# Score matmuls with a selector as the stationary operand, over keys transposed as fp32 pairs, in a decode attention kernel

## The chip, the cores and the metric

The kernel runs on one core of one Trainium2 chip. The metric is the device time of one execution in microseconds. A trace is of one execution: two traces whose loops run the same code differ by 0.12 us per pair, so smaller differences between traces say nothing.

## The reference

Two branches, mixed by a gate. Nearly all the time goes to the attention branch: 2 batches x 32 heads, one query each, 16384 keys of 128 elements.

```python
q = (x @ wq).reshape(B, 1, 32, 128).transpose(0, 2, 1, 3)
scores = einsum("bhqd,bhkd->bhqk", q, k_cache) * 128 ** -0.5
p = softmax(scores)
o = einsum("bhqk,bhkd->bhqd", p, v_cache)
a = o.transpose(0, 2, 1, 3).reshape(B, 1, 4096) @ wo
b = mixer_mlp(x)                      # small: 2 rows through four weights
return g * a + (1 - g) * b            # g = sigmoid(sum(x * gate_w))
```

K and V together are 537 MB; with the weights the kernel reads 572.5 MB.

A warning on "correct": the comparison with the reference says little about the score path, and I don't use it as proof that a re-ordered score layout is right.

## The kernel before: the parts that matter

The kernel is written engine by engine, with semaphores; the code below is abridged to what matters here. The 64 head-batch pairs `i` go one after another. A pair has 4 K pieces and 4 V pieces of 1 MB each, loaded into a ring of 16 slots; a load for a slot is issued by SP once the slot's former piece has been used up. K pieces alternate between two paths (`KPATH = "pd"`).

Path "p" (TensorE): 8 transposes per group, ScalarE evicts the group, and 8 score matmuls with the keys as the stationary operand follow two groups later (`QKLAG = 2`).

```python
for g in range(GPP):                             # 4 groups of 8 rows per piece
    for cc in range(8):                          # waits for the eviction 3 groups before (3 PSUM banks)
        e.transpose(bank_b(bank, cc*128, ...), slot_ap(s, r*DH, (r+1)*DH), ident_bf)
    act: activation(kt_f32(kts), tps_f32(bank), Copy)        # 128 x 512 fp32 words
    pending_qk.append(...); flush_qk(QKLAG)
ring_free[jp] = last transpose                   # the K slot may be loaded again
# issue_qk: 8 x matmul(S_ps[:, c:c+NQ], lhsT=kt(cc), rhs=qsb[:, i:i+NQ], start=True, stop=True)
# after the last group: 2 x activation(ssb, S_ps, Copy)
```

Path "d" (VectorE): `prd = K * qrep` (`qrep` is the pair's query, copied to all 128 partitions) in two instructions, then two reduces over the 128 elements, straight to the scores `ssb`.

The softmax of a pair closes the loop, because the next pair's `qrep` and evictions stand behind this pair's exp in ScalarE's queue:

```python
dve : tensor_reduce(M_P, ssb, max)                        # waits for all four pieces
pool: partition_all_reduce(GMAX, M_P, max)
pool: tensor_scalar(NBIAS, GMAX, -scale, mult)
act : activation(ptile, ssb, Exp, bias=NBIAS, scale=scale, accum_out=L_P)
pool: partition_all_reduce(LSUM, L_P, add)
# then, next pair:  act: qrep copy, evictions ...   dve: prd <- ring, qrep
```

PV matmuls (the product of the softmax with V: 4 columns of `ptile` stationary, 512 columns of V moving) run five pieces behind, on TensorE, between the K groups.

Of the kernel before, what the change touches and what calls it, by code (L numbers as in the profile page):

```python
# [3 lines left out]
F32 = mybir.dt.float32  # L4
BF16 = mybir.dt.bfloat16
# [53 lines left out]
def build_kernel(nc, A_x, A_k_cache, A_v_cache, A_wq, A_wo, B_x, B_w1, B_w2, B_w3, B_w4,  # L59
# [10 lines left out]
    DSPLIT = cfg.get("DSPLIT", 2)  # L70
    PSPLIT = cfg.get("PSPLIT", 4)
    NPRD2 = cfg.get("NPRD2", 2)
    NT = 3
    VG = 4

# [14 lines left out]
    NPC = SK // PKEYS  # L90
    NCH = SK // 128
    GPP = R // 8
    assert NCH + NQ <= 512 and R % VG == 0
    NPB = LAG // NPC + 2
    assert D <= PE_ELEMS and Fdim <= PE_ELEMS and H * DH <= PE_ELEMS
    S_TOK = Sq
# [8 lines left out]
    ident_bf = nc.alloc_sbuf_tensor("ident_bf", [128, 128], BF16)  # L105
    ident_f = nc.alloc_sbuf_tensor("ident_f", [128, 128], F32)
    qsb = nc.alloc_sbuf_tensor("qsb", [128, NPAIR + NQ], BF16)
    ptile = nc.alloc_sbuf_tensor("ptile", [128, NPB * NCH], BF16)
    ssb = nc.alloc_sbuf_tensor("ssb", [128, NPB * NCH], F32)
    st = nc.alloc_sbuf_tensor("st", [128, NPB * 8], F32)  # L110
# [47 lines left out]
    def bank_f(b, c0, c1):  # L158
        return ps[:, b * 512 + c0: b * 512 + c1]

    def bank_b(b, c0, c1):
        return psb[:, b * 1024 + c0: b * 1024 + c1]

    def S_ps(i):
        return bank_f(3 + (i % 2), 0, NCH + NQ)
    qrow_ps = bank_b(0, 512, 640)[0:NPAIR, :]
    qrep_ps = bank_f(7, 0, 128)
    O4_ps = ps[0:VG, 5 * 512: 6 * 512]
    AT_ps = bank_f(6, 0, W)
# [51 lines left out]
    def ring_dma(src_ap, dst_view=None, width=PE_ELEMS):  # L221
# [20 lines left out]
    t_identf = P.op("pool", lambda e: e.affine_select(  # L242
        out=ident_f[:], in_=ident_f[:], compare_op=ALU.not_equal, fill=1.0, base=0,
        pattern=[[-1, 128]], channel_multiplier=1), [t_identf])
    t_ar0 = P.op("pool", lambda e: e.memset(arscr[:], 0.0))
    t_ar0 = P.op("pool", lambda e: e.partition_all_reduce(arscr[:, 1:2], arscr[:, 0:1], channels=128,
                                                         reduce_op=RED.add), [t_ar0])
# [36 lines left out]
    def matmul_T(pieces, ncols, nk, n_out_tiles, out_ps, rhs_fn, extra_waits, width_b=Bsz):  # L284
        waits = [ring_loaded[j] for (j, s, t0, nt) in pieces] + list(extra_waits)
        last = None
        first = True
        for nt_i in range(n_out_tiles):
            for t in range(nk):
                lhs, j = wtile(pieces, ncols, t, nt_i * 128, (nt_i + 1) * 128)  # L290
                is_last = (nt_i == n_out_tiles - 1 and t == nk - 1)
                last = P.op("pe", (lambda e, o=out_ps[:, nt_i * width_b:(nt_i + 1) * width_b], l=lhs,
                                   r=rhs_fn(t), st_=(t == 0), sp_=(t == nk - 1):
                                   e.matmul(o, lhsT=l, rhs=r, start=st_, stop=sp_)),  # L294
                            waits if first else (), track=is_last)
                first = False
        for (j, s, t0, nt) in pieces:
            ring_free[j] = last
        return last
# [3 lines left out]
    w1p = load_weight_rows(B_w1, KT, D, per_piece_D)  # L303
    w2p = load_weight_rows(B_w2, KT, D, per_piece_D)

    t_QT = matmul_T(wqp, H * DH, KT, H, QT_ps, lambda t: xT_bf[:, t * Bsz:(t + 1) * Bsz], [t_xTbf])
    t_qsb = P.op("dve", lambda e: e.tensor_copy(qsb[:, 0:NPAIR], QT_ps), [t_QT])
    off = NPAIR
    while off < NPAIR + NQ:
        wdt = min(NPAIR, NPAIR + NQ - off)  # L310
        t_qsb = P.op("dve", lambda e, off=off, wdt=wdt: e.tensor_copy(qsb[:, off:off + wdt], qsb[:, 0:wdt]),
                     [t_qsb])
        off += wdt
    t_qrowp = P.op("pe", lambda e: e.transpose(qrow_ps, qsb[:, 0:NPAIR], ident_bf[:]), [t_qsb, t_ident])
    t_qrow = P.op("dve", lambda e: e.tensor_copy(qrow[:], qrow_ps), [t_qrowp])
    w3p = load_weight_rows(B_w3, KT, Fdim, max(1, PE_ELEMS // Fdim))

    t = P.op("dve", lambda e: e.tensor_tensor(
        v3(gp[:]), v3(xT_f[:]), gwT_f[:].unsqueeze(2).broadcast_to([128, KT, Bsz]), ALU.mult),
        [t_xTf, t_gwTf])  # L320
# [26 lines left out]
        return t10  # L347

    t_ln1 = layernorm_T(xT_f, t_xTf, ln_s[0])
    lnT = ln_s[0]["out"]  # L350
    t_hT = matmul_T(w1p, D, KT, KT, hT_ps, lambda t: lnT[:, t * Bsz:(t + 1) * Bsz], [t_ln1])
    t_u1 = P.op("act", lambda e: e.activation(u1T[:], hT_ps, ACTF.Gelu_apprx_tanh), [t_hT])
# [33 lines left out]
        stream.append(("V", n))  # L386

    def kpath(n):
        return KPATH[n % len(KPATH)]

    evac_tk = {}
# [42 lines left out]
    def softmax(i):  # L434
# [11 lines left out]
        pooladd_tk[i] = P.op("pool", lambda e: e.partition_all_reduce(  # L446
            stc(j, LSUM), stc(j, L_P), channels=128, reduce_op=RED.add), [exp_tk[i], prev(rl_tk, i, NPB)])

    def issue_qk(gd):
        i, pc, g, n, kts = gd  # L450
        j = i % NPB
        waits = [evac_tk[n]]
        if not qk_started.get(i):
            qk_started[i] = True
            waits += prev_list(sread_tk, i, 2) + [t_qsb]
        last = None
        for cc in range(8):
            c = pc * R + g * 8 + cc
            last = P.op("pe", (lambda e, o=S_ps(i)[:, c:c + NQ], l=kt_ap(kts, cc * 128, (cc + 1) * 128),
                               r=qsb[:, i:i + NQ]: e.matmul(o, lhsT=l, rhs=r, start=True, stop=True)),  # L460
                        waits if cc == 0 else (), track=(cc == 7))
        qk_tk[n] = last
        if g == GPP - 1:
            pe_done.setdefault(i, []).append(pc)
            if len(pe_done[i]) == sum(1 for q in range(NPC) if kpath(i * NPC + q) == "p"):
                for pcq in pe_done[i]:
                    c0 = pcq * R
                    tk = P.op("act", (lambda e, o=S_sb(j)[:, c0:c0 + R], a=S_ps(i)[:, c0:c0 + R]:
                                      e.activation(o, a, ACTF.Copy)), [last, prev(exp_tk, i, NPB)])  # L469
                    sread_tk.setdefault(i, []).append(tk)  # L470
                for tk in list(sread_tk[i]):
                    add_part(i, tk)

    qk_started = {}
    pe_done = {}

    def flush_qk(keep):
# [28 lines left out]
    def finish(i):  # L506
# [17 lines left out]
        if b == Bsz - 1:  # L524
            pending_A.append(h)

    def k3(ap, nr):
        return ap.rearrange("p (r d) -> p r d", d=DH)

    for (kind, n) in stream:  # L530
# [11 lines left out]
        if kind == "K":  # L542
            path = kpath(n)
            if pc == 0 and any(kpath(i * NPC + q) != "p" for q in range(NPC)):
                make_qrep(i)
            if path == "p":
                for g in range(GPP):
                    gn = gcount[0]
                    gcount[0] += 1
                    bank = gn % NT  # L550
                    kts = gn % NKT
                    waits = []
                    if g == 0:
                        waits.append(ring_loaded[jp])
                    if gn >= NT:
                        waits.append(evac_tk[gn - NT])
                    if gn == 0:
                        waits += [t_qsb, t_ident, t_qrow]
                    last = None
                    for cc in range(8):  # L560
                        r = g * 8 + cc
                        last = P.op("pe", (lambda e, o=bank_b(bank, cc * 128, (cc + 1) * 128),
                                           a=slot_ap(s, r * DH, (r + 1) * DH): e.transpose(o, a, ident_bf[:])),  # L563
                                    waits if cc == 0 else (), track=(cc == 7))
                    tT_tk[gn] = last
                    ev = EVAC[gn % len(EVAC)]
                    ew = [tT_tk[gn], prev(qk_tk, gn, NKT)]
                    if ev == "d":
                        evac_tk[gn] = P.op("dve", lambda e, o=kt_f32(kts), a=tps_f32(bank): e.tensor_copy(o, a), ew)
                    else:  # L570
                        evac_tk[gn] = P.op("act", lambda e, o=kt_f32(kts), a=tps_f32(bank):
                                           e.activation(o, a, ACTF.Copy), ew)  # L572
                    pending_qk.append((i, pc, g, gn, kts))
                    flush_qk(QKLAG)
                ring_free[jp] = tT_tk[gcount[0] - 1]
            else:
# [19 lines left out]
                                ([ring_loaded[jp], qrep_tk[i]] + wfree) if q_ == 0 else ())  # L596
                    qrep_users[i].append(last)
                ring_free[jp] = last
                rsd = R // DSPLIT
                red = None  # L600
                for q_ in range(DSPLIT):
                    red = P.op("dve", (lambda e, o=scols[:, q_ * rsd:(q_ + 1) * rsd],
                                       a=k3(dst_ap[:, q_ * rsd * DH:(q_ + 1) * rsd * DH], rsd):
                                       e.tensor_reduce(o, a, AX.X, ALU.add)),  # L604
                               ([last, prev(exp_tk, i, NPB)]) if q_ == 0 else ())
                if path == "d":
                    prd_free[0] = red
                else:
# [4 lines left out]
        else:  # L613
# [3 lines left out]
            last = None  # L617
            ngq = R // VG
            for gq in range(ngq):
                c0 = pc * R + gq * VG  # L620
                is_last = (gq == ngq - 1)
                last = P.op("pe", (lambda e, l=P_ap(j, c0, c0 + VG),
                                   rr=slot_ap(s, gq * VG * DH, (gq + 1) * VG * DH),
                                   st_=(c0 == 0), sp_=(c0 == NCH - VG):
                                   e.matmul(O4_ps, lhsT=l, rhs=rr, start=st_, stop=sp_)),  # L625
                            waits if gq == 0 else (), track=is_last)
            ring_free[jp] = last
# [86 lines left out]
```

## Time and profile before

Median 2014.72 us (2013.1 to 2017.89, 4 runs).

The page's first part: busy time of each engine, with its share of the span.

```profile
span 2011.3 us, 26961 instructions
PE 1100.0 (55%) x11908; PEld 659.2 (33%) x11908; DVE 1176.9 (59%) x675; ACT 394.2 (20%) x971; POOL 72.7 (4%) x207
```

No engine is over 60% busy. The chain that ended last, by engine and by line, says why: a third of the span is "issue", time for which the profile shows no wait.

```profile
DVE 57%; issue 33%; POOL 2%; ACT 2%; PE 2%; DMA 2%; SPq 1%; DVEq 0%; POOLq 0%
DVE prd L595 28%; DVE ssb L604 28%; ACT ptile L443 2%; SPq L231 1%; POOL st L438 1%; DMA ring<-in_A_wq_dram 1%; POOL st L441 1%; DVE st L436 1%; PE ps L625 1%; DMA ring<-in_B_w_dram 1%; PE ps L294 1%; ACT qrep L501 1%; DVEq L50 0%; DVE st L510 0%; POOLq L441 0%
```

The costliest groups (line, engine, operation, out<-in, shape, count | busy us, mean ns of one | idle before and what ended it):

```profile
L595 DVE TENSOR_TENSOR prd<-ring,qrep 128x2048 f32<-128x2048 bf16 x256 | 575.1, 2288 | 716.3 <-ACT qrep L501 709.2
L604 DVE TENSOR_REDUCE ssb<-prd 128x16 f32<-128x2048 f32 x256 | 573.3, 2281 | 4.4
L460 PE MATMUL ps<-qsb,ktr 128*128 128x32 bf16 x4096 | 173.3, 183 | 798.3 <-ACT ktr L572 798.3
L625 PE MATMUL ps<-ring,ptile 128*4 128x512 bf16 x2048 | 595.7, 444 | 21.3 <-ACT ptile L443 21.3
L572 ACT ACTIVATE ktr<-ps 128x512 f32<-128x512 f32 x512 | 277.1, 597 | 211.3 <-PE ps L563 210.5
L563 PE MATMUL ps<-ident_bf,ring 128*128 128x128 bf16 x4096 | 306.9, 234 | 0.0
L441 POOL TENSOR_SCALAR st<-st 128x1 f32<-128x1 f32 x64 | 18.0, 281 | 632.9 <-issue 632.9
```

The last line: GpSimd's little tensor_scalar of 128x1 is idle 632.9 us in front of it, for "issue". At the end of each all-reduce of the maximum, and after each tensor_scalar, the trace has two MODIFY_POOL_CONFIG, 260 in all. These are the lines for them (line, engine, count, duration in ns, first and last start):

```profile
L441 POOLq MODIFY_POOL_CONFIG  x128: 83/83/85, 103.6 to 1985.8; - x128
L446 POOLq MODIFY_POOL_CONFIG  x128: 11/11/11, 113.0 to 1993.5; - x128
```

The way back, from the tensor_scalar to the all-reduce of the sum, is idle for 6.18 us on average, but nothing waits for that one. One pair in the timeline (start us, us, engine line operation, idle before):

```profile
1005.40 0.40 ACT L443 ACTIVATE ptile<-ssb,st 128x128 bf16<-128x128 f32 x1 [15.77 <-POOL st L441]
...
1006.16 4.49 DVE L595 TENSOR_TENSOR prd<-ring,qrep 128x2048 f32<-128x2048 bf16 x2 [11.17 <-ACT qrep L501]
1007.91 0.33 SPq L231 DMA_DIRECT2D ring<-in_A_k_cache_dram  x1
...
1011.45 0.33 SPq L231 DMA_DIRECT2D ring<-in_A_v_cache_dram  x1
...
1021.98 0.28 ACT L469 ACTIVATE ssb<-ps 128x32 f32<-128x32 f32 x2 [1.95 <-PE ps L460]
...
1024.41 0.29 DVE L436 TENSOR_REDUCE st<-ssb 128x1 f32<-128x128 f32 x1
...
1024.80 0.37 POOL L438 PARTITION_ALL_REDUCE st<-st  x1 [12.77 <-DVE st L510]
1036.63 0.26 POOL L441 TENSOR_SCALAR st<-st 128x1 f32<-128x1 f32 x1 [11.46 <-issue]
```

Read it as a loop. Exp at 1005.40; VectorE's four multiplies and reduces; the maximum at 1024.41; the all-reduce; then 11.46 us of nothing; the tensor_scalar at 1036.63 and exp again. TensorE's scores of this pair are copied at 1021.98, 2.4 us before the maximum: that path is not on the chain, but close.

The means over pairs 2 to 61 (the gap, here and below, over 3 to 61), from the trace's instructions and data packets:

| per pair, us | before |
|---|---|
| exp to exp | 30.12 (29.07 to 31.52) |
| exp to end of TensorE's score copy | 15.21 (13.66 to 17.05) |
| exp to end of VectorE's last reduce | 18.88 |
| exp to start of the maximum | 19.02 |
| all-reduce to tensor_scalar ("the gap") | 10.07 |
| exp to end of the last K/V packet | 27.09 |

In the last two pairs, with no load in flight during the gap, it is 6.76 and 7.06 us.

### The profile page before, as it was taken

The numbers are of one execution on the slowest core, as the hardware profiler recorded it, in microseconds if no ns is written. First come the engines' busy times: TensorE is split into PE (matmuls) and PEld (weight loads), VectorE is DVE, ScalarE is ACT, GpSimd is POOL, SyncE is SP. The second block draws the span as 40 slices with busy tenths as digits, with TensorE's granted clock in tenths as the row PEclk, the third lists the DMA queues.
The fourth block names the chain that finished last, engine by engine and source line by source line (L and its number), as shares of the span: only waits on it lengthen the run. The fifth ranks groups of instructions, "written<-read, shape, count | busy, mean of one in ns | idle before, by whom it ended". The sixth has DMA issues, their size and how long they took to land.

```text
span 2011.3 us, 26961 instructions
## 1 busy us (share of the span) xinstructions
PE 1100.0 (55%) x11908; PEld 659.2 (33%) x11908; DVE 1176.9 (59%) x675; ACT 394.2 (20%) x971; POOL 72.7 (4%) x207
## 2 busy tenths in 40 slices
PE   2454564564564564565465564565465465465466
PEld 2432332332332342332242332343243233233233
DVE  0375575575575575575575575575575575575573
ACT  1121121121121121121121121121121122121221
POOL 0010000000000000000000000000000000000000
PEclk9977777776776777777776777776777786777787
DMA  9997766776776776776776776776776776776670
GB/s 384 407 420 280 308 274 263 310 283 260 309 280 262 305 287 253 313 282 269 296 292 251 310 282 257 309 299 255 298 305 253 289 313 252 288 301 264 282 277 1
DMA packets 86645, 574.29 MB, mean 286 GB/s; under 512 B 9216, under 2 KB 9216, under 8 KB 19968
## 3 DMA queue, kind: packets, MB, share of 16 engines
q1 hardware_dynamic: 86528, 572.57, 71.6%
q8 instruction: 93, 1.52, 0.3%
q14 instruction: 24, 0.20, 0.0%
HBM read 572.53 MB, written 0.00 MB: 285 GB/s over the span
## 4 chain that ended last, share of the span: by engine, by line
DVE 57%; issue 33%; POOL 2%; ACT 2%; PE 2%; DMA 2%; SPq 1%; DVEq 0%; POOLq 0%
DVE prd L595 28%; DVE ssb L604 28%; ACT ptile L443 2%; SPq L231 1%; POOL st L438 1%; DMA ring<-in_A_wq_dram 1%; POOL st L441 1%; DVE st L436 1%; PE ps L625 1%; DMA ring<-in_B_w_dram 1%; PE ps L294 1%; ACT qrep L501 1%; DVEq L50 0%; DVE st L510 0%; POOLq L441 0%
## 5 line engine op out<-in xcount | busy, mean ns | idle before, releaser
L595 DVE TENSOR_TENSOR prd<-ring,qrep 128x2048 f32<-128x2048 bf16 x256 | 575.1, 2288 | 716.3 <-ACT qrep L501 709.2
L460 PE MATMUL ps<-qsb,ktr 128*128 128x32 bf16 x4096 | 173.3, 183 | 798.3 <-ACT ktr L572 798.3
L625 PE MATMUL ps<-ring,ptile 128*4 128x512 bf16 x2048 | 595.7, 444 | 21.3 <-ACT ptile L443 21.3
L604 DVE TENSOR_REDUCE ssb<-prd 128x16 f32<-128x2048 f32 x256 | 573.3, 2281 | 4.4
L460 PEld LDWEIGHTS ps<-qsb,ktr 128*128 128x128 bf16 x4096 | 146.1, 101 | 879.2 <-ACT ktr L572 808.9
L572 ACT ACTIVATE ktr<-ps 128x512 f32<-128x512 f32 x512 | 277.1, 597 | 211.3 <-PE ps L563 210.5
L563 PE MATMUL ps<-ident_bf,ring 128*128 128x128 bf16 x4096 | 306.9, 234 | 0.0
L563 PEld LDWEIGHTS ps<-ident_bf,ring 128*128 128x128 bf16 x4096 | 259.0, 105 | 39.5 <-issue 35.0
L625 PEld LDWEIGHTS ps<-ring,ptile 128*4 128x4 bf16 x2048 | 170.9, 93 | 303.2 <-issue 150.5
L443 ACT ACTIVATE ptile<-ssb,st 128x128 bf16<-128x128 f32 x64 | 25.7, 401 | 937.3 <-POOL st L441 937.3
L516 PE MATMUL ps<-ident_f,od 4*128 4x1 f32 x512 | 68.7, 251 | 19.1 <-ACT od L513 16.6
L513 ACT ACTIVATE od<-ps 4x512 f32<-4x512 f32 x64 | 37.6, 587 | 184.5 <-PE ps L625 184.5
L516 PEld LDWEIGHTS ps<-ident_f,od 4*128 4x128 f32 x512 | 63.3, 190 | 26.6 <-ACT od L513 26.6
L438 POOL PARTITION_ALL_REDUCE st<-st x64 | 25.5, 398 | 856.0 <-DVE st L510 799.8
L469 ACT ACTIVATE ssb<-ps 128x32 f32<-128x32 f32 x128 | 18.3, 195 | 120.7 <-PE ps L460 120.7
L441 POOL TENSOR_SCALAR st<-st 128x1 f32<-128x1 f32 x64 | 18.0, 281 | 632.9 <-issue 632.9
L446 POOL PARTITION_ALL_REDUCE st<-st x64 | 25.7, 401 | 396.4 <-issue 307.2
L521 ACT ACTIVATE otb<-ps,st 128x1 bf16<-128x1 f32 x64 | 16.9, 264 | 74.5 <-PE ps L516 72.2
L436 DVE TENSOR_REDUCE st<-ssb 128x1 f32<-128x128 f32 x64 | 18.3, 286 | 11.6 <-ACT ssb L469 3.0
L372 DVE TENSOR_TENSOR bT<-x1T_f,ps 128x16 f32<-128x16 f32 x1 | 0.2, 172 | 35.6 <-PE ps L294 35.6
L501 ACT ACTIVATE qrep<-ps 128x128 bf16<-128x128 f32 x64 | 16.4, 256 | 19.6 <-PE ps L499 19.6
L510 DVE RECIPROCAL st<-st 128x1 f32<-128x1 f32 x64 | 9.8, 153 | 14.3 <-POOL st L446 14.3
(71 smaller groups left out, 118.3 us busy)
## 6 DMA issues: line engine op xcount, KB each, us to landing
ring<-in_A_k_cache_dram SPq DMA_DIRECT2D x256, 1024.0 KB, 7.8
ring<-in_A_v_cache_dram SPq DMA_DIRECT2D x256, 1024.0 KB, 7.6
ring<-in_B_w_dram SPq DMA_DIRECT2D x11, 1024.0 KB, 19.6
ring<-in_A_wq_dram SPq DMA_DIRECT2D x8, 1024.0 KB, 11.9
wor<-in_A_wo_dram SPq DMA_DIRECT2D x32, 256.0 KB, 7.7
ring<-in_B_w_dram SPq DMA_DIRECT2D x8, 896.0 KB, 15.3
x<-in_A_x_dram SPq DMA_DIRECT2D x1, 4.0 KB, 1.5
gw<-in_gate_w_dram SPq DMA_DIRECT2D x1, 2.0 KB
```

The costliest lines, as they stand in the source:

```text
L436: mx_tk[i] = P.op("dve", lambda e: e.tensor_reduce(stc(j, M_P), S_sb(j), AX.X, ALU.max), part_tk[i] + [prev(poolmax_tk, i, NPB)])
L438: poolmax_tk[i] = P.op("pool", lambda e: e.partition_all_reduce(stc(j, GMAX), stc(j, M_P), channels=128, reduce_op=RED.max), [mx_tk[i], pr ...
L441: nbias_tk[i] = P.op("pool", lambda e: e.tensor_scalar(stc(j, NBIAS), stc(j, GMAX), -scale, None, ALU.mult), [poolmax_tk[i], prev(exp_tk, ...
L443: exp_tk[i] = P.op("act", lambda e: e.activation(P_ap(j, 0, NCH), S_sb(j), ACTF.Exp, bias=stc(j, NBIAS), scale=scale, accum_out=stc(j, L_P ...
L460: r=qsb[:, i:i + NQ]: e.matmul(o, lhsT=l, rhs=r, start=True, stop=True)),
L513: ocopy_tk[i] = P.op("act", lambda e: e.activation(odj, O4_ps, ACTF.Copy), [pvlast_tk[i], prev(osum_tk, i, NPB)])
L516: osum_tk[i] = P.op("pe", (lambda e, m=m: e.matmul(oT_ps, lhsT=odj[:, m * 128:(m + 1) * 128], rhs=ident_f[0:VG, m:m + 1], start=(m == 0), ...
L563: a=slot_ap(s, r * DH, (r + 1) * DH): e.transpose(o, a, ident_bf[:])),
L572: e.activation(o, a, ACTF.Copy), ew)
L595: last = P.op(eng, (lambda e, o3=o3, i3=i3, qb3=qb3: e.tensor_tensor(o3, i3, qb3, ALU.mult)), ([ring_loaded[jp], qrep_tk[i]] + wfree) if q ...
L604: e.tensor_reduce(o, a, AX.X, ALU.add)),
L625: e.matmul(O4_ps, lhsT=l, rhs=rr, start=st_, stop=sp_)),
```

## The change

The intent: fewer, larger TensorE instructions for the scores. Two neighbouring bf16 rows are seen as one row of fp32 words, so one fp32 transpose moves two rows: 4 transposes per group for 8. The eviction untangles even and odd elements. The query then becomes the stationary operand, in a 32-column window that puts it into one pair of output rows ("selector"), and 512 key columns move; 2 accumulating matmuls per group for 8. The scores come out as 32x512 and need a ScalarE copy, four transposes and two strided copies. Because the score columns now come in another order, VectorE's reduces (4 smaller ones per piece) and PV's operands are strided to match. The last six K pieces all go to TensorE (`TAILP = 6`). The diff is abridged.

```diff
-for cc in range(8): e.transpose(bank_b(...), slot_ap(s, r*DH, (r+1)*DH), ident_bf)
+for t4 in range(4): e.transpose(bank_f(bank, t4*128, ...), slot_ap(s, r*DH, (r+2)*DH).bitcast(F32), ident_f)
-evac: activation(kt_f32(kts), tps_f32(bank), Copy)
+evac: activation(kt "j par tp", bank_b "j (tp par) -> j par tp", Copy)     # 1024 bf16, source step 2
-for cc in range(8): matmul(S_ps(i)[:, c:c+NQ], lhsT=kt(cc), rhs=qsb[:, i:i+NQ], start=True, stop=True)
+for par in range(2):
+    matmul(ST_ps(i), lhsT=wbuf[:, base+30-2*Gp : base+62-2*Gp], rhs=kt(par*512, (par+1)*512),
+           start=(first and par == 0), stop=(is_last_group and par == 1))
 # after a pair's last group
-2 x activation(ssb, S_ps, Copy)
+activation(stsb, ST_ps(i), Copy)                       # 32 x 512
+4 x transpose(Sp_ps, stsb(t4), ident_f[0:32, 0:32])
+2 x activation(ssb strided, Sp_ps strided, Copy)
 # VectorE piece
-for q_ in range(DSPLIT): tensor_reduce(ssb[16], prd[16*128])               # 2 x 2048
+for g_ in range(GPP):    tensor_reduce(ssb strided [4, 2], prd[8*128])     # 4 x 1024
 def kpath(n):
+    if n >= NKP - TAILP: return "p"
     return KPATH[n % len(KPATH)]
+make_w(i): 2 x activation(wbuf window, qe/qo columns, Copy)                # after qrep, each pair
 ... (start-up: selectors psel, qe, qo; PV operands strided; order of the start-up)
```

Within the loop, the order of the instructions around them is the same as before.

## The prediction

> **What bounds it now.** 64 head-batch pairs run one after another; the pairs 2 to 61 take 30.1 us each (29.1 to 31.5, start of one exp to the next). The chain of waits shows the loop: exp, qrep (ScalarE), then VectorE 18.1 us (two K pieces, each 2 multiplies and 2 reduces of 2.24 us), max reduce, partition all-reduce on GpSimd, an "issue" gap before the GpSimd tensor_scalar of 10.05 us on average, tensor_scalar, exp. [...] the trace has two MODIFY_POOL_CONFIG per pair, and gaps of 6.8 and 7.1 us in the last two pairs, where no cache traffic is left. So I read 3 us of the gap as contention with K/V loads, which saturate the queues for some 22 us per pair and end 7.3 us into the gap.
>
> TensorE and ScalarE are off the chain, but not by much: the last PE-path score copy ends 15.2 us after exp (13.7 to 17.0), VectorE's maximum starts at 19.0. Slack 3.8 us, in odd pairs only 2 to 3.5.
>
> **What changes, per pair.**
> - VectorE: 4 reduces of 1024 for 2 of 2048. [...] +0.43 us, on the chain.
> - ScalarE eviction: 128x1024 bf16 for 128x512 fp32. The trace has 597 ns[...]. It delays the first scores after exp, with two small selector copies, by 0.7 us, and the second piece by 0.5.
> - TensorE scores: 2 matmuls of 512 columns for 8 of 32. PV's 512-column matmul takes 0.43 us cold, 0.236 warm: 0.86/0.47 us per group for 0.43/0.36. About +1.5 us.
> - Transposes: 4 fp32 for 8 bf16. The lone fp32 transpose in the tail takes 0.38 us, the bf16 one 0.32, [...] no large change (-0.5 to +1 us).
> - New before the maximum: 32x512 copy, four transposes, two strided copies instead of two plain ones: +1.4 us.
>
> The PE path thus ends near 19.6 us after exp (odd pairs 21, even 18) against VectorE's 19.45: it becomes the later one in odd pairs. The maximum comes 0.4 us (even) to 2 us (odd) later, 1.2 on average. Slots come free about 1.5 us later too, so the loads end later and the gap doesn't shrink. About +1.35 us x 61 = +82 us. The tail (last three VectorE pieces moved to TensorE) I expect to cost 10 us rather than save, as 16 evictions and their groups plus PV exceed VectorE's 19 us. Start-up: unchanged.
>
> **Predicted: 2105 us, 2045 to 2190.** Faster by over 2%: 0.03; within 2%: 0.17; slower: 0.80.
>
> **What would show it.** Right: reduces of about 1.2 us; [...] period near 31.4 us; the maximum's wait in odd pairs ended by ScalarE's score copy, not VectorE's reduce; gap still near 10 us; granted clock little changed. Wrong: PE path still ending before VectorE (then only +30 us); gap below 9 us.
>
> **What would make it wrong.** [...] load timing that changes the gap by 1 us (60 us in all); a tail that gains.

## The result

Median 2073.31 us (2064.23 to 2081.49, 10 runs) against 2015.13 us (16 runs) of the kernel before: ratio 1.0293, 95% interval 1.0276 to 1.0311. The change is slower. Ratios here are the mean time of one kernel's fast runs over that of the other's from the same rounds, so not quite the ratio of the medians quoted.

The profile after, the same parts of the page:

```profile
span 2068.7 us, 17839 instructions
PE 1262.2 (61%) x7119; PEld 631.0 (31%) x7119; DVE 1165.9 (56%) x917; ACT 666.9 (32%) x1177; POOL 74.1 (4%) x213
...
DVE 39%; issue 33%; PE 17%; ACT 6%; POOL 2%; DMA 2%; SPq 1%; POOLq 0%; DVEq 0%
DVE ssb L685 19%; DVE prd L676 19%; PE ps L710 7%; PE ps L514 5%; PE ps L643 2%; ACT ktr L653 2%; ACT ptile L477 2%; SPq L242 1%; POOL st L472 1%; PE ps L588 1%; DMA ring<-in_A_wq_dram 1%; DVE st L470 1%; POOL st L475 1%; DMA ring<-in_B_w_dram 1%; PE ps L314 1%
...
L676 DVE TENSOR_TENSOR prd<-ring,qrep 128x2048 f32<-128x2048 bf16 x250 | 561.6, 2288 | 724.7 <-ACT wbuf L491 718.2
L514 PE MATMUL ps<-ktr,wbuf 128*32 128x512 bf16 x1048 | 347.8, 439 | 666.2 <-ACT ktr L653 666.2
L685 DVE TENSOR_REDUCE ssb<-prd 128x8 f32<-128x1024 f32 x500 | 574.8, 1211 | 4.3
L653 ACT ACTIVATE ktr<-ps 128x1024 bf16<-128x1024 bf16 x524 | 500.2, 1024 | 186.8 <-PE ps L643 186.2
L710 PE MATMUL ps<-ring,ptile 128*4 128x512 bf16 x2048 | 541.4, 412 | 16.1 <-ACT ptile L477 16.1
L643 PE MATMUL ps<-ident_f,ring 128*128 128x128 f32 x2096 | 317.6, 298 | 0.0
...
L475 POOL TENSOR_SCALAR st<-st 128x1 f32<-128x1 f32 x64 | 17.4, 272 | 651.4 <-issue 651.4
```

A third fewer instructions (17839 for 26961), and TensorE is busier: the score matmuls cost 347.8 us for 173.3, and the half as many transposes 317.6 for 306.9. ScalarE's evictions went from 277.1 to 500.2 us. The chain's TensorE part (17%, 2% before) is not the end of the kernel alone: a_tail0 below, without the tail move, still has 16%. It is there because in some pairs the score copy now ends after VectorE, and the chain then runs through TensorE for the whole pair.

One pair in the timeline:

```profile
1028.97 0.40 ACT L477 ACTIVATE ptile<-ssb,st 128x128 bf16<-128x128 f32 x1 [12.68 <-POOL st L475]
...
1029.73 4.49 DVE L676 TENSOR_TENSOR prd<-ring,qrep 128x2048 f32<-128x2048 bf16 x2 [11.62 <-ACT wbuf L491]
1030.78 1.04 PE L514 MATMUL ps<-ktr,wbuf 128*32 128x512 bf16 x2 [11.37 <-ACT ktr L653]
1031.75 1.12 PE L643 MATMUL ps<-ident_f,ring 128*128 128x128 f32 x4
1032.89 0.33 SPq L242 DMA_DIRECT2D ring<-in_A_k_cache_dram  x1
...
1035.80 0.33 SPq L242 DMA_DIRECT2D ring<-in_A_v_cache_dram  x1
...
1047.30 0.29 ACT L536 ACTIVATE ssb<-ps 128x32 f32<-128x32 f32 x2 [0.52 <-PE ps L527]
...
1048.22 0.29 DVE L470 TENSOR_REDUCE st<-ssb 128x1 f32<-128x128 f32 x1
...
1058.54 0.26 POOL L475 TENSOR_SCALAR st<-st 128x1 f32<-128x1 f32 x1 [9.57 <-issue]
```

Here too the score copy (1047.30 to 1047.59) still ends before the maximum starts (1048.22). But SP issues the first load 3.92 us after exp, for 2.51 before, since the eviction and the first score group ahead of it got longer; the first V load comes at 6.83 us, for 6.05.

| per pair, us (means of pairs 2 to 61) | before | after |
|---|---|---|
| exp to exp | 30.12 | 30.73 |
| exp to end of TensorE's score copy | 15.21 | 18.86 (later than VectorE in 18 of 60 pairs) |
| exp to end of VectorE's last reduce | 18.88 | 19.11 |
| exp to start of the maximum | 19.02 | 19.33 |
| the gap | 10.07 | 10.35 |
| exp to issue of the 1st / 2nd / 8th cache load | 2.49 / 5.92 / 16.76 | 3.92 / 7.42 / 20.39 |
| exp to end of the last K/V packet | 27.09 | 28.50 |

The 57.4 us between the two profiled spans divide as follows, from the exp times in the two traces: +4.1 us up to the second pair's exp (there the maximum waits 7.03 us for the score copy), +36.4 us in the 60 pairs of the loop, +17.4 us in the last two pairs (33.3 and 38.0 us for 26.8 and 27.1), -0.5 us after them.

The last two pairs, where all or nearly all pieces are on TensorE: VectorE's maximum waits for the score copies.

```profile
2004.63 0.29 DVE L470 TENSOR_REDUCE st<-ssb 128x1 f32<-128x128 f32 x1 [15.05 <-ACT ssb L536]
...
2042.93 0.29 DVE L470 TENSOR_REDUCE st<-ssb 128x1 f32<-128x128 f32 x1 [37.94 <-ACT ssb L536]
```

### The profile page after: what moved, and what is told of

Its sections match the earlier page's. It is cut to its first block, busy times and chain, and to the rows that moved or that the text cites. A ratio compares the mean times of both kernels' runs of the same rounds, so it can differ in the third digit from the quotient of the medians.

```text
span 2068.7 us, 17839 instructions
## 1 busy us (share of the span) xinstructions
PE 1262.2 (61%) x7119; PEld 631.0 (31%) x7119; DVE 1165.9 (56%) x917; ACT 666.9 (32%) x1177; POOL 74.1 (4%) x213
## 4 chain that ended last, share of the span: by engine, by line
DVE 39%; issue 33%; PE 17%; ACT 6%; POOL 2%; DMA 2%; SPq 1%; POOLq 0%; DVEq 0%
DVE ssb L685 19%; DVE prd L676 19%; PE ps L710 7%; PE ps L514 5%; PE ps L643 2%; ACT ktr L653 2%; ACT ptile L477 2%; SPq L242 1%; POOL st L472 1%; PE ps L588 1%; DMA ring<-in_A_wq_dram 1%; DVE st L470 1%; POOL st L475 1%; DMA ring<-in_B_w_dram 1%; PE ps L314 1%
## 5 line engine op out<-in xcount | busy, mean ns | idle before, releaser
L514 PE MATMUL ps<-ktr,wbuf 128*32 128x512 bf16 x1048 | 347.8, 439 | 666.2 <-ACT ktr L653 666.2
L685 DVE TENSOR_REDUCE ssb<-prd 128x8 f32<-128x1024 f32 x500 | 574.8, 1211 | 4.3
L653 ACT ACTIVATE ktr<-ps 128x1024 bf16<-128x1024 bf16 x524 | 500.2, 1024 | 186.8 <-PE ps L643 186.2
L710 PE MATMUL ps<-ring,ptile 128*4 128x512 bf16 x2048 | 541.4, 412 | 16.1 <-ACT ptile L477 16.1
L514 PEld LDWEIGHTS ps<-ktr,wbuf 128*32 128x32 bf16 x1048 | 82.2, 99 | 794.7 <-ACT ktr L653 718.4
L643 PE MATMUL ps<-ident_f,ring 128*128 128x128 f32 x2096 | 317.6, 298 | 0.0
L643 PEld LDWEIGHTS ps<-ident_f,ring 128*128 128x128 f32 x2096 | 244.2, 150 | 116.0 <-issue 111.6
L522 ACT ACTIVATE stsb<-ps 32x512 f32<-32x512 f32 x64 | 37.6, 587 | 104.6 <-PE ps L514 104.6
L527 PE MATMUL ps<-ident_f,stsb 32*128 32x32 f32 x256 | 27.5, 227 | 43.7 <-ACT stsb L522 43.7
L527 PEld LDWEIGHTS ps<-ident_f,stsb 32*128 32x128 f32 x256 | 20.5, 136 | 75.3 <-ACT stsb L522 75.3
L475 POOL TENSOR_SCALAR st<-st 128x1 f32<-128x1 f32 x64 | 17.4, 272 | 651.4 <-issue 651.4
```

The costliest lines, as they stand in the source:

```text
L475: nbias_tk[i] = P.op("pool", lambda e: e.tensor_scalar(stc(j, NBIAS), stc(j, GMAX), -scale, None, ALU.mult), [poolmax_tk[i], prev(exp_tk, ...
L514: e.matmul(ST_ps(i), lhsT=l, rhs=r, start=st_, stop=sp_)),
L527: tk = P.op("pe", (lambda e, t4=t4: e.transpose(Sp_ps[:, t4 * 32:(t4 + 1) * 32], stj[:, t4 * 128:(t4 + 1) * 128], ident_f[0:32, 0:32])), ( ...
L643: e.transpose(o, a, ident_f[:])),
L653: evac_tk[gn] = P.op("act", lambda e, o=o_pl, a=a_pl: e.activation(o, a, ACTF.Copy), ew)
L685: red = P.op("dve", (lambda e, o=o, a=a: e.tensor_reduce(o, a, AX.X, ALU.add)), ([last, prev(exp_tk, i, NPB)]) if g_ == 0 else ())
```

## The experiments

The diffs below are abridged. The theory after the result: (1) the tail move costs its 17 us; (2) the loop loses, in part, because VectorE's added reduces and the later score copy delay the maximum; (3) and, in part, because slots are freed later, so the loads end later and stretch the gap. The rival for the loop: only the maximum counts, and the gap is GpSimd's own.

### a_tail0: the tail move undone

```diff
-    TAILP = cfg.get("TAILP", 6)
+    TAILP = cfg.get("TAILP", 0)
```

> The changed kernel with the last three VectorE pieces left on VectorE (TAILP 0). Theory: the tail move costs what the traces show for the last two pairs (33.3 + 38.0 us for 26.8 + 27.1, so 17 us): about 2056 us, ratio to the kernel before 1.0205. Rival, the intent of the change (the tail gets shorter by the move): 2080 us or more.

2052.09 us, ratio 1.0187 (1.0168 to 1.0207), as expected. The last two pairs take 27.8 and 28.0 us again. So the tail move cost about 20 us of the 58, and 1.9% remain.

### b_dsplit4: smaller VectorE instructions in the kernel before

```diff
-    DSPLIT = cfg.get("DSPLIT", 2)
+    DSPLIT = cfg.get("DSPLIT", 4)
```

> The kernel before with four reduces of 1024 per piece instead of two of 2048, nothing else. Theory: VectorE is on the loop, each piece's reduces take 4.60 for 4.48 us, so 0.25 us per pair and 15 us in all if the gap keeps its length, 9 us if a later maximum finds part of the loads already done: ratio 1.0045 to 1.0075. Rival (the loop is held by the end of the loads, not by VectorE): no change, ratio 0.999 to 1.002.

2021.92 us, ratio 1.0046 (1.003 to 1.0061). My description of the edit was wrong: the option splits the multiplies too, so the maximum came 0.50 us later, not 0.25 (19.52 us after exp). A pair grew by only 0.14 us, since the gap shrank from 10.07 to 9.69 us. A later maximum is mostly forgiven. For the change's 0.31 us that makes (an estimate, in proportion) 0.09 us per pair, 5 us in all.

### a_red2: two reduces per piece again, in the changed kernel

```diff
-for g_ in range(GPP):  # out offset 8*pc + 2*g_, [[32,4],[1,2]]; in 8 rows, "t=4, h=2"
+for g_ in range(2):    # out offset 8*pc + 64*g_, [[32,2],[1,8]]; in 16 rows, "t=2, h=8"
 # PV of the VectorE pieces reads V rows at step 8*DH instead of 2*DH
```

> The changed kernel with the VectorE pieces' score columns laid out so that two reduces of 2048 per piece do again (PV reads them to match). Theory: 9 to 15 us come back of the changed kernel's 2073, ratio 1.0215 to 1.025. Rival (TensorE's path sets the maximum anyway): under 3 us back, ratio 1.028 or more.

2065.37 us, ratio 1.0256 (1.0231 to 1.028): 0.4% back, below the range expected, and the intervals of this and the change overlap. VectorE is done at 18.89 again, but now the score copy ends later than VectorE in 39 of 60 pairs, and the maximum starts at 19.23 for 19.33.

### a_ev32: the cheap eviction again

```diff
-o_pl = kt_ap(kts) "j (par tp) -> j par tp";  a_pl = bank_b(bank) "j (tp par) -> j par tp"
+o_pl = kt_f32(kts);                          a_pl = tps_f32(bank)
-rhs = kt_ap(kts, par*512, (par+1)*512)
+rhs = kt_ap(kts) "j (tp two) -> j two tp" [:, par, :]
```

> The changed kernel with the eviction as contiguous 512 fp32 words again, and the score matmuls reading every second bf16 column. Theory: the eviction takes 0.60 for 1.02 us; the first scores and the first free K slot after exp come 0.4 us sooner, the score path ends 1 us sooner, the two all-TensorE pairs at the end gain up to 6 us: 2052 to 2062 us, ratio 1.019 to 1.023. Rival (a moving operand at a step of two is read at half rate): score matmuls near 0.86 us cold, the time above 2080 us.

2060.27 us, ratio 1.0243 (1.0221 to 1.0265), 0.5% better than the change; the time lies within the range expected, the ratio just above it. The eviction takes 596 ns for 1024, and the score matmul, though it now reads every second element, 444 ns for 439: untangling in the matmul's operand is free here, in the eviction it is not. The loads move earlier (first packet 4.39 us after exp for 4.81, last packet 27.84 for 28.50), and yet the loop of this trace is no shorter: 30.74 us per pair for 30.73, gap 10.43 for 10.35. What its trace gains, it gains in the last two pairs (32.2 and 35.8 us for 33.3 and 38.0). This speaks against cause (3) in the changed kernel; the traced execution (2067.56 us) is one of the slower of the five, so the trace doesn't account for the whole 0.5% either.

### b_half: half of the loads

```diff
-jp, s = ring_dma(kv_src(cache, i, pc))
+if n < 16: jp, s = ring_dma(kv_src(cache, i, pc))
+else:      jp, s = ring_dma(kv_src(cache, i, pc)[:, 0:PE_ELEMS//2], width=PE_ELEMS//2)
```

> The kernel before, but from the 17th cache piece of each cache on only the first half of every K and V piece is loaded (wrong result on purpose); all compute stays. Theory [...]: the loads of a pair are over before the gap, it falls to 6.8 to 7.3 us in all pairs, a pair takes 27 us, about 1825 us in all. Rival (the gap is GpSimd's own, whatever the loads do): gap near 10 us, 2000 us or more.

1852.75 us, ratio 0.9188 (0.9158 to 0.9218), 1.5% above what was expected, and far from the rival's 2000. The loads end 21.97 us after exp, 2.2 us into the gap, and the gap is 7.36 us on average for 10.07. Here is that wait in the list of waits (who waited <- for what: us in total, times, longest), of the kernel before:

```profile
POOL st L441 <- issue: 632.9, 64, 11.5
```

And of the kernel with half the loads:

```profile
POOL st L441 <- issue: 472.3, 64, 8.9
```

The compute is the same in both; so at least 2.7 us of the gap are due to the loads. The rest remains without loads: in the last two pairs of the eleven runs with this gap it is 6.7 to 7.7 us. (The result is wrong, yet passed the comparison: the warning above.)

### b_delay: the loads later, nothing else

One ScalarE copy of 1.36 us after qrep, in the kernel before.

```diff
 qrep_tk[i] = act: activation(qrep, qrep_ps, Copy)
+act: activation(dly[1408], ident_f broadcast, Copy)
```

> The kernel before with one added ScalarE copy of 1408 elements (about 1.3 us) per pair, right after qrep and before the first evictions; nothing else changes. VectorE's chain is not touched, and the score path (15.2 us after exp) stays 2.5 us before VectorE's maximum. It only lets TensorE free the first K slot 1.3 us later, as the change does (first load 4.8 for 3.4 us after exp). Theory (what remains of the loss in the loop comes from the later loads, which reach further into the gap): last load 1 us or more later, gap 0.3 to 0.6 us longer, 20 to 37 us in all, ratio 1.010 to 1.018. Rival (the loop is VectorE and GpSimd only): ratio 0.999 to 1.003.

2060.45 us, ratio 1.0227 (1.0203 to 1.0251): more than the range expected, and at least as much as the whole change without its tail. The maximum starts at 19.02 us, exactly as before, and the score copy never comes near it (16.47). On the way to the maximum only the loads moved: first, second and eighth issue at 3.75, 7.05 and 18.00 us (before 2.49, 5.92, 16.76), last packet at 28.23 for 27.09, gap 10.81 for 10.07. One pair in its timeline:

```profile
1025.92 0.40 ACT L444 ACTIVATE ptile<-ssb,st 128x128 bf16<-128x128 f32 x1 [15.37 <-POOL st L442]
...
1026.48 1.36 ACT L507 ACTIVATE dly<-ident_f 128x1408 bf16<-128x1408 f32 x1
...
1029.69 0.33 SPq L232 DMA_DIRECT2D ring<-in_A_k_cache_dram  x1
...
1044.92 0.29 DVE L437 TENSOR_REDUCE st<-ssb 128x1 f32<-128x128 f32 x1
...
1057.14 0.26 POOL L442 TENSOR_SCALAR st<-st 128x1 f32<-128x1 f32 x1 [11.46 <-issue]
```

This rules out the rival for the kernel before: 1.36 us of ScalarE per pair, at a place where the chain of waits doesn't pass, cost 45 us.

### a_lag3, a_lag3_tail0, b_lag3: the K slot freed first

Holding the score matmuls back one more group lets TensorE finish a piece's transposes, and free its slot, before the first score group.

```diff
-    QKLAG = cfg.get("QKLAG", 2)
+    QKLAG = cfg.get("QKLAG", 3)
```

> The changed kernel with the score matmuls held back one group more (QKLAG 3), so that TensorE transposes the fourth group, and frees the K slot, before the first score matmuls after exp. No work is added or removed. Theory (load timing): first load 3.8 for 4.8 us after exp, last load 1 us earlier, gap 0.4 to 0.6 us shorter: 2035 to 2048 us, ratio 1.010 to 1.017. Rival (the loop's loss is the later maximum and ScalarE's added work): the score path ends no earlier, so ratio 1.026 to 1.032.

> The same, and the last three VectorE pieces left on VectorE. Theory: both losses are additive, 20 us less than the run with the lag alone: 2013 to 2028 us, ratio 1.000 to 1.007, so within 1% of the kernel before.

> The kernel before with the same lag of 3. Here the score group is short (0.42 us), so the first load comes only 0.4 to 0.5 us sooner. Theory: 0.2 to 0.3 us per pair, ratio 0.990 to 0.995. Rival: 0.999 to 1.002.

- a_lag3: 2061.05 us, ratio 1.0228 (1.0203 to 1.0253), a miss: 12 us better than the change for 25 to 38 expected. The first load was issued at 2.95 us for 3.92, as planned. But the second one moved only from 7.42 to 7.03, the eighth not at all (20.39), and the last packet from 28.50 to 28.22. The first load came sooner, but the pause after it widened from 3.50 to 4.08 us. So an earlier start of the burst of loads is not enough. That an earlier end would be is not shown: in a_ev32 it came 0.66 us sooner without a shorter loop.
- a_lag3_tail0: 2045.78 us, ratio 1.0153 (1.0133 to 1.0172). The same small gain over a_tail0's 1.0187; it does not bring the change level with the kernel before, as I had expected.
- b_lag3: 2005.04 us, ratio 0.995 (0.9935 to 0.9965), as expected: last packet 26.94 for 27.09, gap 9.87 for 10.07. A gain of 0.5% over the kernel before for one number, at the edge of the range.

### The gap against the loads, over all runs

For the eleven profiles that keep the tensor_scalar on GpSimd, I set the mean time from exp to the tensor_scalar against the mean time from exp to the last K/V packet:

| run | last packet, us | maximum, us | tensor_scalar, us |
|---|---|---|---|
| b_half | 21.97 | 19.02 | 27.13 |
| b_lag3 | 26.94 | 19.02 | 29.64 |
| before | 27.09 | 19.02 | 29.84 |
| b_dsplit4 | 27.11 | 19.52 | 29.97 |
| b_delay | 28.23 | 19.02 | 30.58 |
| after | 28.50 | 19.33 | 30.44 |
| a_ev32 | 27.84 | 19.25 | 30.44 |
| a_lag3 | 28.22 | 19.33 | 30.36 |
| a_lag3_tail0 | 28.25 | 19.37 | 30.28 |
| a_tail0 | 28.56 | 19.35 | 30.31 |
| a_red2 | 28.61 | 19.23 | 30.40 |

A straight line through all eleven is 16.0 + 0.51 x (last packet), off by at most 0.27 us (0.41 instead of 0.51 without b_half). It takes the change's 1.41 us to 0.7 us per pair; measured were 0.61. But the line is carried by the runs of the kernel before. The six runs of the changed kernel, with last packets from 27.84 to 28.61 us, show no such relation (correlation -0.16). Pair by pair within one run it is loose too (correlation of gap and last packet about 0.6 before, -0.1 after). So this is a statement on means; for the changed kernel the share of the loads in its loss is inferred from the kernel before, and the way in which the loads stretch the gap is not shown.

### b_nb, a_nb, a_nb_tail0: the multiply off GpSimd

If the gap is there because an all-reduce and a tensor_scalar alternate on GpSimd, moving the one multiply to ScalarE should remove it.

```diff
-nbias_tk[i] = P.op("pool", tensor_scalar(NBIAS, GMAX, -scale, None, ALU.mult), ...)
+nbias_tk[i] = P.op("act", activation(NBIAS, GMAX, ACTF.Copy, scale=-scale), ...)
```

> The kernel before with the multiply of the maximum by minus the scale moved from GpSimd to ScalarE, so that GpSimd runs only all-reduces in the loop[...]. Theory: the gap goes; VectorE's loop is 20.3 us, the loads need 21.5 to 22 us per pair and become the limit: 1470 to 1560 us. Rival (the gap is a wait for loads, or the all-reduce itself is slow): over 1900 us.

> The changed kernel with the same move of the one multiply from GpSimd to ScalarE. Theory: loads limit here too, so the two versions come within 3% of each other, the changed one behind by its tail (17 us) and more where its longer score path (18.9 us after exp) can no longer hide: 1490 to 1600 us.

> The changed kernel [...] (the multiply on ScalarE) and without the tail move. Theory: the 10 us by which it trailed the kernel before with the same edit are the tail alone, so 1392 to 1399 us, ratio 0.690 to 0.694, the same as the kernel before with that edit.

| run | us | ratio (95%) | exp to exp, us | last two pairs, us |
|---|---|---|---|---|
| b_nb | 1395.37 | 0.6921 (0.6905 to 0.6937) | 20.28 | 20.0, 20.6 |
| a_nb | 1405.10 | 0.6971 (0.6954 to 0.6988) | 20.27 | 23.7, 28.1 |
| a_nb_tail0 | 1395.87 | 0.6925 (0.6913 to 0.6937) | 20.26 | 20.2, 21.2 |

The trace has 4 MODIFY_POOL_CONFIG instead of 260, the gap is gone (0.27 us from the end of the all-reduce to exp), and the kernel takes 31% less time. b_nb and a_nb both came in below the ranges expected, as the loads run at 420 GB/s and a pair's 8.4 MB plus its share of wo need only 20.3 us; a_nb_tail0 lies in its range. That the gap belongs to the alternation of the two instructions is thus shown; what GpSimd does during it, no view of the profile shows. The page of b_nb (GB/s in 40 slices, and the share of the DMA engines' time):

```profile
PE 1080.1 (77%) x11908; PEld 648.9 (46%) x11908; DVE 1176.9 (84%) x675; ACT 405.6 (29%) x1035; POOL 52.8 (4%) x143
...
DVE  0169999999999999999988989898898998889884
...
DMA  9999999999999999999999999999999999999993
GB/s 369 402 418 420 420 419 420 421 419 420 421 419 421 420 420 420 420 420 420 420 420 421 419 420 420 420 420 420 420 420 420 420 419 421 420 420 420 419 417 152
...
q1 hardware_dynamic: 86528, 572.57, 99.2%
```

The queues are busy for 99.2% of the span. With the loads as the limit the change's loop costs nothing: a pair takes the same time, and without the tail move the two versions are equal.

## Why the prediction was right, point by point

The range held (2105 predicted, 2045 to 2190; 2073 measured), in part by luck and by a wide range: by the prediction's own tests the main term failed. The period was to be near 31.4 us (30.73), the granted clock little changed (0.75 to 0.82 in the loop), and the TensorE path later than VectorE (in 42 of 60 pairs it was not, the case for which the prediction itself allowed only +30 us). The terms of the sum, in the prediction's order:

- "The loop: exp, qrep, VectorE, maximum, all-reduce, gap": right. "I read 3 us of the gap as contention with K/V loads": b_half shows 2.7 us. In the pair shown of the kernel before the queues were busy for 97% of the time from 1010 to 1025 us, at 381 GB/s. Of the MODIFY_POOL_CONFIG there are four per pair, two after the all-reduce of the maximum and two after the tensor_scalar. Where no loads run the gap is 6.76 and 7.06 us, on the way back it is 6.18 us on average, and b_nb shows that without the alternation it is gone (0.27 us from the all-reduce to exp).
- "VectorE: +0.43 us": too much; the amount was my estimate. The four reduces take 4.60 us for 4.48 (0.12 per piece, 0.06 us for each extra instruction), 0.24 us per pair. And less of it counts than the prediction took: b_dsplit4 delayed the maximum by 0.50 us and lost 0.14.
- "ScalarE eviction: 128x1024 bf16 for 128x512 fp32": 1024 ns for 597, with the bf16 source in PSUM read at a step of two. The delays put on it, 0.7 and 0.5 us, were my estimate.
- "TensorE scores 0.86/0.47 us per group": in the timeline a group takes 1.03 us early in a pair and 0.61 later, for 0.42 and 0.37 before. Busy over the kernel it is 347.8 us for 173.3. "Cold" and "warm" are the PV groups early and late in a pair: in the pair shown of the kernel before, eight matmuls took 3.38 us from 1008.05 (granted clock 0.55) and 1.89 us from 1021.87 (1.00).
- "Transposes: no large change": right. Twelve fp32 transposes take 1.53 us, the 24 bf16 ones that they replace 1.51.
- "New before the maximum: +1.4 us" and "the PE path ends near 19.6 us": 18.86. Odd pairs 19.2 for 21 predicted, even ones 18.5 for 18. TensorE was granted more clock (0.82 for 0.75 in the loop, in which it was busy for 62% of the time, for 56%), and its PV matmuls took 411 ns for 443 (the first PV group of the pair shown 2.15 us, at a granted clock of 0.88, for 3.38 us at 0.55). So "it becomes the later one in odd pairs" happened in 18 of 60 pairs only (16 of the 30 odd ones), and "the maximum comes 1.2 us later" was 0.31: the mis-sized term of the sum.
- "Slots come free about 1.5 us later too, so the loads end later": right, 1.41 us, and b_delay shows that in the kernel before a delay of the loads by 1.1 to 1.3 us is by itself worth at least the loop's loss (1.0227 for a_tail0's 1.0187). The prediction gave it the smaller role, "the gap doesn't shrink"; the gap grew by 0.29 us although the maximum came later.
- "+1.35 us x 61 = +82 us": 0.61 x 60 = 36.4. "The tail I expect to cost 10 us": 17.4, as the last pair needs 29.8 us from exp to its score copy. "Start-up: unchanged": +4.1, the second pair's score path.

So the direction and the parts of the mechanism were right and the sum was 32 us too high. The weights within it were wrong: the delayed maximum was over-sized four times, the tail was under-sized, and so, as b_delay suggests, was the load timing.

What stays open: how K/V traffic lengthens the gap, how the loop's 36 us divide between the later maximum and the later loads, why a_ev32's earlier loads shortened nothing, and why the change's gap (10.35 us) is shorter than b_delay's (10.81) although their last packets come at nearly the same time (the change's later maximum, as in b_dsplit4, may be part of it; not tested).

## What to carry to other kernels

Fewer and larger TensorE instructions were no gain here, where TensorE was busy for 55% of the span, and they were not even cheaper (347.8 us of score matmuls for 173.3); cost an instruction by what it delays (the next slot to come free, the next load), not only by the chain of waits. When an engine stands idle for "issue" in front of a tiny instruction, look at what it did just before: alternating GpSimd's all-reduce with a tensor_scalar went with two idle stretches per pair (10.07 us on the loop and 6.18 us off it), and moving one 128x1 multiply to ScalarE took 31% off a kernel on which the diff under study moved 3%. Test such a suspicion by changing one thing that the chain doesn't show; b_delay and b_half settled more than the repairs of the change did, though what they show of the kernel before need not hold in full for the changed one.
